# Packed attention with an ELU feed-forward: bit-shifted weights, a refitted planner and split operands

## The chip, the cores and the metric

The kernel runs on one core of a Trainium2 chip. The metric is the device time of one execution in microseconds (us). Before the change three runs took 710.84, 713.93 and 712.98 us; their median is 712.98 us. A smaller time is better.

The core has five engines that run side by side, each through its own instructions in a fixed order: PE (TensorE, the matrix multiplier), DVE (VectorE), ACT (ScalarE), POOL (GpSimd) and SP (SyncE, which here only issues transfers). PEld is PE's loading of the stationary operand.

## The reference

Attention runs twice: 32 packed queries `p` read 576 keys and values, and then the 576 queries `q` read the 32 packed results. A feed-forward with an ELU follows.

```python
# q, k, v: (8, 8, 576, 64) float32; p: (8, 8, 32, 64) float32
def sm_attn(qq, kk, vv):
    s = scale * np.matmul(qq, kk.transpose(0, 1, 3, 2))
    a = np.exp(s - np.max(s, axis=-1, keepdims=True))
    a = a / (np.sum(a, axis=-1, keepdims=True) + 1e-09)
    return np.matmul(a, vv)
p_packed = sm_attn(p, k, v)
out = sm_attn(q, p_packed, p_packed)
x = out.transpose(0, 2, 1, 3).reshape(4608, 512)
h = x @ w_in                                   # w_in: (512, 2048) float64
g = np.where(h > 0.0, h, np.exp(np.minimum(h, 0.0)) - 1.0)
return (g @ w_out).astype(np.float32)          # w_out: (2048, 512) float64
```

The weights arrive as float64, since they are drawn and divided by a float64 root. The chip gets them as pairs of 32-bit words and makes float32 of them itself.

## The kernel before

**Work.** A batch is 576 tokens; there are eight. `w_in` is cut into 16 column blocks of 128 and `w_out` into 16 row blocks, both numbered by `f`. A *step* is one (batch, window, f): the two windows of a batch take 256 and 320 tokens, the 64 odd tokens of an even batch being paired with those of the next batch. A step computes `h` for 128 hidden units (PE), ReLU of -h and exp (ACT), the ELU (DVE), splits the result (ACT cast, DVE subtract), and multiplies it by block `f` of `w_out` (PE, called the *out product* below), accumulating in PSUM.

**h without x.** The packed result `ppT` of a batch is multiplied by `w_in` once (`mstep`, L796), giving `m`; a step then multiplies `m` by the second attention's weights `a` (L1278, L1285, L1048), so `x` is never formed.

**Split operands.** Most products take each float32 operand as a high and a low float32r part and add three products (high x high, high x low, low x high). Where an operand is kept whole, one float32 product is made instead. Before the change this is so for `h` in batches 0 and 1 for `f < 4` (`H_PLAIN = [0, 1]`, L1278, operands `m_hi` and `af`, which lies in the tiles named `k` and `q`) and for the out products of batches 0 and 1 for `f < 4` (`F_PLAIN = 4`, L1395, weights in `w_words`).

**Strassen.** From batch 2's second window to batch 7's first (`strassen_pair`, L1187 and L1048) two steps form a pair, whose out product is a 2x2 block product with seven instead of eight block products. Its sums of weights are made once (`strassen_weights`), stored in `sw_dram` and loaded again for each window. In `S_PLAIN` and `S_PLAINS` stand the pairs of a window that do the plain product with twelve 512-wide matmuls instead of 21 of 256.

**Conversion** (`weights`). Each of the 32 weight blocks (128 x 512 float64) is loaded into one of three `raw` buffers. Before, DVE cuts out the exponent field (`ex`, L312), ACT makes a power of two from it (L319) and a sign from the high word (`sg`, L324), DVE masks the mantissa (`mi`, L327), adds the low word (L333), multiplies power and sign (L340) and multiplies mantissa by that (L350). A `w_out` block is then split (ACT cast, DVE subtract, L363).

**Order.** Every piece of work is an `op` with an urgency, a cost for each engine it may run on, and what it needs. `schedule()` runs through simulated time: whenever an engine is free, the most urgent op that is ready gets it. `GAP` is what is added between two instructions of an engine, `LAG` how much later a result counts as ready. The order so found is written out, engine by engine, and on the chip each engine keeps to it. The first two batches are visited in the order `VISITS` of (batch, window, first f, last f), so that the weight blocks are needed one after another; 64 steps belong to them. `FIRST` orders the first transfers; `T_ATT`, `TM` and the like say how many steps ahead of its use a batch's attention and `mstep` are due; `LOOK` and `LOOK_S` say how many steps the out product stands behind its `h`.

## Time and profile before

| | |
|---|---|
| runs | 710.84, 712.98, 713.93 us; median 712.98 |
| profiled execution, first to last instruction (span) | 710.4 us; its own device time is not given beside it |
| PE busy | 687.2 us, 97% of the span |
| PEld busy | 573.6 us, 81% |
| DVE busy | 587.7 us, 83% |
| ACT busy | 448.1 us, 63% |
| POOL busy | 19.4 us, 3% |
| mean granted PE clock | 0.996 |
| bytes moved | 140.19 MB, 197 GB/s |

Busy time of an engine is time in which at least one of its instructions runs; neighbours overlap by some tens of nanoseconds, so the busy time of a stretch is less than the sum of its instructions. A float32 matmul stands in the trace as two records, a float32r matmul as one. Stages differ much: up to about 31 us the first transfers and the first attention run, up to about 165 us the first two batches with all conversions, then two windows of batch 2 and the Strassen part, and from about 668 us the last window.

### The profile page before, as it was taken

How to read it: one execution, taken by the hardware profiler on the slowest of the kernel's cores; microseconds unless marked ns; L12 is line 12 of the kernel's file. 1: busy time of each engine (PE TensorE's matmuls, PEld its weight loads, DVE VectorE, ACT ScalarE, POOL GpSimd, SP SyncE). 2: the span in 40 equal slices, each digit the busy share in tenths (PEclk: the TensorE clock that was granted, in tenths of full speed). 3: DMA queues.
4: the chain of work that ended last, by engine and by line, in shares of the span. 5: the costliest groups of instructions: out<-in, count | busy, mean ns of one | idle time of the engine just before them, and what ended most of it. 6: DMA issues, size and time to landing. Idle time of an engine off the chain costs nothing.

```text
span 710.4 us, 15186 instructions
## 1 busy us (share of the span) xinstructions
PE 687.2 (97%) x5688; PEld 573.6 (81%) x5688; DVE 587.7 (83%) x1430; ACT 448.1 (63%) x963; POOL 19.4 (3%) x27
## 2 busy tenths in 40 slices
PE   2799999999999999999999999999999999999997
PEld 1444588887777888899889998889888999899986
DVE  6999998888998889776898799866798889977563
ACT  5777788887666666665466555756556655655532
POOL 0000002111021000000000000000000000000000
PEclk9999999999999999999999999999999999999999
DMA  9846555645748845646867897566867887754600
GB/s 354 291 152 216 165 177 117 140 86 124 215 94 208 285 137 179 179 145 195 297 195 260 280 306 230 185 185 203 266 220 243 278 257 226 210 189 138 204 31 30
DMA packets 72553, 140.19 MB, mean 197 GB/s; under 512 B 7200, under 2 KB 16672, under 8 KB 72224
## 3 DMA queue, kind: packets, MB, share of 16 engines
q1 hardware_dynamic: 69456, 133.72, 58.2%
q0 software_dynamic: 3024, 5.51, 5.5%
q8 instruction: 45, 0.74, 0.4%
q14 instruction: 28, 0.23, 0.1%
HBM read 116.92 MB, written 22.28 MB: 196 GB/s over the span
## 4 chain that ended last, share of the span: by engine, by line
PE 93%; DMA 3%; DVE 2%; ACT 1%; issue 0%; SPq 0%; ACTq 0%
PE psum L1187 29%; PE psum L1048 19%; PE psum L1285 8%; PE psum L1409 6%; PE psum L1410 5%; PE psum L1412 5%; PE psum L1007 5%; PE psum L796 4%; PE psum L1395 4%; PE psum L1278 2%; DMA kvq<-in_qT 2%; PE psum L650 2%; PE psum L624 1%; PE psum L695 1%; DMA k<-in_kT 1%; PE psum L554 1%
## 5 line engine op out<-in xcount | busy, mean ns | idle before, releaser
L1187 PE MATMUL psum<-sw,g 128*128 128x256 f32 x816 | 126.0, 282 | 0.0
L1187 PEld LDWEIGHTS psum<-sw,g 128*128 128x128 f32 x816 | 109.9, 188 | 6.5 <-issue 4.7
L1048 PE MATMUL psum<-a_hi,m_hi 128*128 128x320 f32 (+1 forms) x320 | 97.3, 304 | 0.0
L1048 PE MATMUL psum<-a_lo,m_hi 128*128 128x320 f32 (+1 forms) x320 | 95.4, 298 | 0.0
L1048 PE MATMUL psum<-a_hi,m_lo 128*128 128x320 f32 (+1 forms) x320 | 95.3, 298 | 0.0
L1130 DVE TENSOR_TENSOR g<-w,g 128x896 fp32r<-128x896 f32 (+1 forms) x80 | 82.0, 1026 | 13.6 <-ACT g L284 13.1
L284 ACT CAST g<-w 128x896 fp32r<-128x896 f32 (+1 forms) x80 | 71.2, 890 | 23.9 <-DVE w L1121 15.0
L1187 PE MATMUL psum<-wo_a,g 128*128 128x256 f32 (+1 forms) x390 | 72.8, 318 | 0.0
L1121 DVE TENSOR_TENSOR w<-w 128x128 f32<-128x128 f32 (+1 forms) x204 | 68.1, 334 | 5.0
L1060 ACT ACTIVATE e<-psum 128x320 f32<-128x320 f32 x96 | 42.0, 437 | 44.9 <-PE psum L1048 40.1
L1048 PEld LDWEIGHTS psum<-a_hi,m_hi 128*128 128x128 f32 x320 | 60.4, 189 | 11.3 <-ACT e L1063 5.0
L1292 ACT ACTIVATE e<-psum 128x256 f32<-128x256 f32 (+1 forms) x96 | 38.6, 404 | 43.8 <-PE psum L1285 30.2
L1187 PEld LDWEIGHTS psum<-wo_a,g 128*128 128x128 f32 x390 | 58.7, 189 | 8.0 <-issue 2.6
L1048 PEld LDWEIGHTS psum<-a_lo,m_hi 128*128 128x128 f32 x320 | 60.4, 189 | 1.6
L1048 PEld LDWEIGHTS psum<-a_hi,m_lo 128*128 128x128 f32 x320 | 60.4, 189 | 0.0
L1187 PE MATMUL psum<-wo_b,g 128*128 128x256 f32 (+1 forms) x366 | 59.6, 290 | 0.0
L1187 PEld LDWEIGHTS psum<-wo_b,g 128*128 128x128 f32 x366 | 50.9, 188 | 5.3 <-issue 3.1
L1285 PE MATMUL psum<-a_hi,m_hi 128*128 128x256 f32 (+1 forms) x160 | 49.2, 307 | 0.1
L1055 DVE SCALAR_TENSOR_TENSOR w<-e,psum 128x256 f32<-128x256 f32 x96 | 39.6, 413 | 11.5 <-ACT e L1063 11.1
L1063 ACT ACTIVATE e<-e 128x320 f32<-128x320 f32 x96 | 45.3, 472 | 2.5
L1285 PE MATMUL psum<-a_lo,m_hi 128*128 128x256 f32 (+1 forms) x160 | 46.4, 290 | 0.0
L1285 PE MATMUL psum<-a_hi,m_lo 128*128 128x256 f32 (+1 forms) x160 | 46.4, 290 | 0.0
(140 smaller groups left out, 1436.3 us busy)
## 6 DMA issues: line engine op xcount, KB each, us to landing
sw<-sw_dram SPq DMA_DIRECT2D x272, 256.0 KB, 3.6
raw<-in_w_in SPq DMA_DIRECT2D x16, 512.0 KB, 3.9
kvq<-in_v SPq DMA_DIRECT2D x16, 512.0 KB, 5.2
raw<-in_w_out SPq DMA_DIRECT2D x16, 512.0 KB, 3.5
kvq<-in_kT SPq DMA_DIRECT2D x14, 576.0 KB, 5.0
kvq<-in_qT SPq DMA_DIRECT2D x14, 576.0 KB, 5.9
sw_dram<-sw SPq DMA_DIRECT2D x28, 256.0 KB, 4.1
out<-part POOLq DMA_DIRECT2D x21, 256.0 KB, 5.3
```

The costliest lines, as they stand in the source:

```text
L284: (nc.scalar.copy if e == "ACT" else nc.vector.tensor_copy)(out=out, in_=in_)
L1007: nc.tensor.matmul(acc.t, lhsT=gh.t[:, p * P:(p + 1) * P], rhs=wo(f, q), start=f == n == 0, stop=f == NF - 1 and n == 2,)
L1048: nc.tensor.matmul(ps, lhsT=m_b[p].t[:, g, o:o + P], rhs=st.a.t[q][:, g, cols], start=(n == 0), stop=(n == 3 * G - 1),)
L1055: nc.vector.scalar_tensor_tensor(out=out, in0=e_, scalar=-1.0, in1=ps, op0=ALU.add, op1=ALU.max)
L1060: nc.scalar.activation(out=out, in_=ps, func=AF.Relu, scale=-1.0)
L1063: nc.scalar.activation(out=x, in_=x, func=AF.Exp, scale=-1.0)
L1121: nc.vector.tensor_tensor(out=out, in0=x, in1=y, op=o)
L1130: nc.vector.tensor_tensor(out=g_b.all[:, 7 * P:(7 + b1 - b0) * P], in0=blocks(b0, b1), in1=g_b.all[:, :(b1 - b0) * P].bitcast(F32), op=ALU ...
L1187: nc.tensor.matmul(a.t[:, at * H:at * H + rhs.shape[-1]], lhsT=operand(blk, p), rhs=rhs, start=a.first == u and n == k == 0, stop=a.final ...
L1285: nc.tensor.matmul(ps_b.t[:, :n_tok], lhsT=m_b[x].t[:, g, o:o + P], rhs=st.a.t[y][:, g, cols], start=(n == 0), stop=(n == 3 * G - 1),)
L1292: nc.scalar.activation(out=e_b.t[:, :n_tok], in_=ps_b.t[:, :n_tok], func=AF.Relu, scale=-1.0)
L1409: nc.tensor.matmul(a.t, lhsT=g_b.t[0][:, t], rhs=wo(f, 0), start=first, stop=False)
```

## The change

- **Conversion.** A float64's high word, read as float32 and multiplied by 2^-112 on `field`, and the low word scaled on `tail`, are both `scaled` ops that may run on ACT or DVE. `size` shifts the first left by three bits and ors in the second; `signed` ors in the sign bit of the high word and writes the result. Both are DVE instructions on integers. The instructions at L312, L319, L324, L327, L333, L340 and L350 fall away.
- **Split operands.** `F_PLAIN` goes from 4 to 0 and `H_PLAIN` from `[0, 1]` to `[0]`. All out products are split; `h` is whole for batch 0 and `f < 4` alone.
- **Strassen plain pairs.** `S_PLAIN` becomes empty, and `S_PLAINS` lists the windows: there are 13 plain pairs instead of 12 (the new one is pair 4 of batch 6's first window).
- **Planner.** `GAP` and `LAG` are changed; a result needed on the engine that makes it counts as ready when the engine is free. Visits, first transfers and all urgencies get new values. Some bookkeeping of the planner is faster, with no effect on the order.

Counted over the whole program, the matmuls change like this: 36 float32 matmuls of 512 columns (L1395) fall away, and 108 float32r ones of 512 columns come; 8 of 256 and 8 of 320 columns (float32, L1278) fall away, and 24 of 256 and 24 of 320 (float32r) come; 21 of 256 columns become 12 of 512 in the new plain pair. On DVE 160 conversion instructions become 64; 16 steps get a subtraction that they did not have. On ACT 64 conversion instructions stay 64. SP issues 268 loads of `sw` instead of 272.

```diff
-    T_ATT, T_ATT1 = [11.5, 13.5, 14.0, 15.0, 16.0, 16.0], [-12, -11, -11, -10, -10, -9]
-    FIRST = "i0 i1 i2 i3 k v o0 o1 q".split()
-    F_PLAIN, H_PLAIN = 4, [0, 1]
-    S_PLAIN = [0, 7]
+    T_ATT = [9.0, 13.5, 14.0, 15.0, 16.0, 20.0]
+    FIRST = "i0 i1 o0 k i3 v o1 q".split()
+    F_PLAIN = 0
+    H_PLAIN = [0]
+    S_PLAIN = []
...
-    GAP = {"PE": 0.0, "DVE": -0.03, "ACT": 0.02, "DMA": 0.0, "POOL": 0.0, "CTL": 0.0}
-    LAG = {"PE": 0.15, "DVE": 0.1, "ACT": 0.12, "DMA": 2.2, "POOL": 5.0, "CTL": 0.0}
+    GAP = {"PE": 0.0, "DVE": -0.08, "ACT": -0.1, "DMA": 0.0, "POOL": 0.0, "CTL": 0.0}
+    LAG = {"PE": 0.2, "DVE": 0.05, "ACT": 0.05, "DMA": 2.2, "POOL": 5.0, "CTL": 0.0}
...
+                for x, needs in o.next:
+                    x.wait -= 1
+                    if needs:
+                        x.ready = max(x.ready, idle_at[e] if list(x.on) == [e] else o.end)
...
+        def scaled(e, out, in_, by):
+            if e == "ACT":
+                nc.scalar.activation(out=out, in_=in_, func=AF.Copy, scale=by)
+            else:
+                nc.vector.tensor_scalar(out=out, in0=in_, scalar1=by, scalar2=None, op0=ALU.mult)
...
+        def field(e):
+            scaled(e, mi_b.t.bitcast(F32), words()[1].bitcast(F32), 2.0 ** -112)
+        def tail(e):
+            scaled(e, rd_b.t, words()[0], 0.9369 * 2.0 ** -29)
+        def size(e):
             nc.vector.scalar_tensor_tensor(
-                out=mi_b.t.bitcast(F32), in0=words()[0], scalar=2.0 ** -32, in1=mi_b.t,
-                op0=ALU.mult, op1=ALU.add,
+                out=mi_b.t, in0=mi_b.t, scalar=3, in1=rd_b.t,
+                op0=ALU.logical_shift_left, op1=ALU.bitwise_or,
             )
...
             nc.vector.scalar_tensor_tensor(
-                out=out, in0=ms, scalar=2.0 ** -20, in1=pw, op0=ALU.mult, op1=ALU.mult
+                out=out.bitcast(U32), in0=top, scalar=0x80000000, in1=bits,
+                op0=ALU.bitwise_and, op1=ALU.bitwise_or,
             )
...
-        x = op(prio, {"DVE": 0.42}, exponent, [ld], take=[ex_b], use=[raw])
-        s = op(prio, {"ACT": 0.66}, sign, [ld], take=[sg_b], use=[raw])
-        p = op(prio, {"ACT": 0.72}, power, [x], use=[ex_b])
-        m = op(prio, {"DVE": 0.42}, mantissa, [ld], take=[mi_b], use=[raw])
-        w = op(prio, {"DVE": 0.69}, whole, [m], use=[raw, mi_b])
-        g = op(prio, {"DVE": 0.42}, signed, [p, s], use=[ex_b, sg_b])
+        x = op(prio, {"ACT": 0.66, "DVE": 0.42}, field, [ld], take=[mi_b], use=[raw])
+        y = op(prio, {"ACT": 0.66, "DVE": 0.42}, tail, [ld], take=[rd_b], use=[raw])
+        y = op(prio, {"DVE": 0.69}, size, [x, y], use=[mi_b, rd_b])
```

While conversions are left, the planner adds 2 us to the cost of DVE when it chooses between ACT and DVE; all 64 `field` and `tail` instructions stand on ACT.

**Where the order moves, DVE, about 23 to 31 us.** This is batch 0's second softmax, first half: maximum (`mx`), difference, ACT's exp, sum (`sm`), scaling, and the transpose into the tile `k` that the first `h` reads. Before, from the sign product of a conversion on:

```order
L340 TENSOR_TENSOR ex<-ex,sg 128x512
L363 TENSOR_TENSOR wo_a<-w_words,wo_a 128x512
L723 TENSOR_REDUCE sm_374<-tmp 128x18
L523 TENSOR_REDUCE mx<-psum 128x1
L726 TENSOR_SCALAR sm_374<-sm_374 128x18
L729 RECIPROCAL sm_374<-sm_374 128x18
L531 TENSOR_SCALAR nb<-mx 128x1
L523 TENSOR_REDUCE mx<-psum 128x1
L732 TENSOR_TENSOR tmp<-tmp,sm_374 128x576
L531 TENSOR_SCALAR nb<-mx 128x1
L350 SCALAR_TENSOR_TENSOR w_words<-mi,ex 128x512
L745 STREAM_TRANSPOSE k_404<-tmp 128x2x288
```

The same place now:

```order
L340 SCALAR_TENSOR_TENSOR mi<-mi,rd 128x512
L350 SCALAR_TENSOR_TENSOR w_in_sb<-raw,mi 128x4x128
L721 TENSOR_REDUCE sm_310<-tmp 128x18
L724 TENSOR_SCALAR sm_310<-sm_310 128x18
L727 RECIPROCAL sm_310<-sm_310 128x18
L730 TENSOR_TENSOR tmp<-tmp,sm_310 128x576
L743 STREAM_TRANSPOSE k_344<-tmp 128x2x288
L521 TENSOR_REDUCE mx<-psum 128x1
L529 TENSOR_SCALAR nb<-mx 128x1
```

The transpose has moved ahead of batch 1's two maxima, and fewer conversion instructions stand in the softmax.

**PE, about 34 to 42 us**: the end of batch 1's first attention (L650, L676) and the first out products. Before:

```order
L650 MATMUL psum<-kvq,tmp 32x64 x40
L1278 MATMUL psum<-k_404,m_hi 128x256 x2
L676 MATMUL psum<-ident,pp 128x128
L1395 MATMUL psum<-w_words,g 128x512 x2
L1278 MATMUL psum<-k_404,m_hi 128x256 x2
```

Now:

```order
L648 MATMUL psum<-kvq,tmp 32x64 x40
L1282 MATMUL psum<-k_344,m_hi 128x256 x2
L674 MATMUL psum<-ident,pp 128x128
L1282 MATMUL psum<-k_344,m_hi 128x256 x2
L794 MATMUL psum<-w_in_sb,ppT 32x256 x8
L1413 MATMUL psum<-wo_a,g 128x512
L1414 MATMUL psum<-wo_a,g 128x512
```

Step 0's out product (L1395 before, L1413 and the rows behind it now) has moved behind the `h` of step 3 and an `mstep`, and consists of split products.

**ACT, among steps 19 to 22**, where a conversion's instructions are `sg` and `ex` before, `mi` and `rd` now. Before:

```order
L1292 ACTIVATE e<-psum 128x320
L284 CAST wo_b<-mi 128x512
L1298 ACTIVATE e<-e 128x320
L319 ACTIVATE ex<-ex,ebias 128x512
L1292 ACTIVATE e<-psum 128x320
L284 CAST g<-e 128x256
L1298 ACTIVATE e<-e 128x320
L324 ACTIVATE sg<-raw 128x512
```

Now:

```order
L1296 ACTIVATE e<-psum 128x320
L1302 ACTIVATE e<-e 128x320
L322 ACTIVATE mi<-raw 128x512
L301 CAST wo_b<-mi 128x512
L301 CAST g<-e 128x256
L322 ACTIVATE rd<-raw 128x512
L1296 ACTIVATE e<-psum 128x320
L1302 ACTIVATE e<-e 128x320
L322 ACTIVATE mi<-raw 128x512
L322 ACTIVATE rd<-raw 128x512
```

More conversion work stands between the ReLUs of two steps than before: the blocks are converted further ahead of their use.

More of the change, by code (lines that the diff above doesn't have):

```diff
@@ L149, in __init__ @@
             self.ring, self.make, self.n, self.users, self.t = ring, make, n, [], None
+            self.free = False
         def released(self, now):
-            return all(u.end is not None and u.end <= now for u in self.users)
+            self.free = self.free or all(u.end is not None and u.end <= now for u in self.users)
+            return self.free
     class Op:
@@ L172, in schedule @@
     def schedule():
+        for o in ops:
+            o.wait, o.ready, o.next = len(o.deps) + len(o.after), 0.0, []
+        for o in ops:
+            for d in o.deps:
+                d.next.append((o, True))
+            for d in o.after:
+                d.next.append((o, False))
         todo = sorted(ops, key=lambda o: (o.prio, o.n))
         idle_at = {e: 0.0 for e in GAP}
-        now, out, mode = 0.0, [], None
+        now, out, mode, converted = 0.0, [], None, 0
+        conv = set(conv_ops)
         def engine_for(o):
-            if any(d.end is None for d in o.after) or any(
-                d.end is None or d.end > now for d in o.deps
-            ):
+            if o.wait or o.ready > now:
                 return None
@@ L212, in schedule @@
                 todo.remove(o)
+                converted += o in conv
                 break
@@ L378, in weights @@
         last = op(
-            prio, {"DVE": 0.69}, product, [w, g], take=take,
-            use=[mi_b, ex_b] + [b for b in words_b if b not in take],
+            prio, {"DVE": 0.69}, signed, [y], take=take,
+            use=[raw, mi_b] + [b for b in words_b if b not in take],
             after=[w_ready[False, f - 1]] if words_b and f % 2 else [],
@@ L902, in strassen @@
         return S_FIRST <= (b, win) < (B - 1, 1)
+    s_needs = [
+        next((i for i, (b, win, _) in enumerate(order) if strassen(b, win) and u not in plain_in(b, win)), None)
+        for u in range(NF // 2)
+    ]
     def s_need(u):
-        return next((i for i, (b, win, _) in enumerate(order) if strassen(b, win) and u not in plain_in(b, win)), None)
+        return s_needs[u]
     def strassen_weights(u):
```

87 lines of the change are left out of this document (40 added, 47 removed), and 7 rows, old and new, of the table VISITS.

## The prediction

> **What bounds the kernel now.** I read the page's busy times and its chain first, to see which engine sets the end.
>
> ```profile
> span 710.4 us, 15186 instructions
> ...
> PE 687.2 (97%) x5688; PEld 573.6 (81%) x5688; DVE 587.7 (83%) x1430; ACT 448.1 (63%) x963; POOL 19.4 (3%) x27
> ...
> PE 93%; DMA 3%; DVE 2%; ACT 1%; issue 0%; SPq 0%; ACTq 0%
> ```
>
> PE is idle for 710.4 - 687.2 = 23.2 us only, and the chain runs through PE for 93% of the span. So a stage's matmuls, and not DVE's 83%, should set its length. Stretches of time show whether that holds everywhere (columns: stretch and length, then PE, PEld, DVE, ACT busy with their instructions).
>
> ```profile
> 0.00:31.30 31.30, 13.28 (x228) 7.98 (x229) 25.15 (x60) 19.93 (x39) 0.69 (x6) 0.97 0.94 354
> ...
> 34.90:62.45 27.55, 27.27 (x197) 13.21 (x185) 26.13 (x59) 19.16 (x43) 0.00 (x0) 1.00 0.59 192
> 62.45:84.10 21.65, 21.50 (x95) 11.51 (x80) 20.60 (x44) 18.35 (x39) 0.00 (x0) 1.00 0.54 170
> 84.10:124.50 40.40, 40.40 (x249) 32.67 (x248) 36.00 (x89) 33.24 (x81) 3.67 (x4) 1.00 0.53 145
> ...
> 165.00:260.00 95.00, 94.23 (x836) 74.70 (x834) 84.60 (x205) 61.70 (x159) 8.78 (x10) 1.00 0.65 182
> 260.00:660.00 400.00, 399.96 (x3514) 355.68 (x3514) 332.68 (x823) 241.32 (x474) 0.00 (x0) 1.00 0.70 221
> 660.00:710.40 50.40, 46.47 (x289) 41.33 (x287) 26.04 (x69) 19.35 (x48) 0.00 (x0) 0.98 0.23 79
> ```
>
> Of PE's 23.2 idle us, 18.0 lie ahead of 31.3 us and 3.9 in the last stretch. In the 400 us of the Strassen part there is none, so nothing but less PE work shortens that. From 34.9 to 84.1 us (steps 0 to 15) two engines are full together: PE 48.8 and DVE 46.7 of 49.2 us. That is where the change does most, and the question is which of the two sets the pace afterwards.
>
> **PE's work.** Prices come from the chain in order of time (start, length, line, records); a float32 matmul is two records.
>
> ```profile
> 48.78 1.72 PE psum L1395 x4
> 50.50 1.08 PE psum L1278 x4
> ...
> 68.12 0.86 PE psum L1278 x4
> ...
> 302.18 2.79 PE psum L1187 x12
> ...
> 318.28 1.75 PE psum L1048 x12
> ...
> 359.42 1.43 PE psum L1048 x12
> ...
> 405.50 2.47 PE psum L1187 x21
> ```
>
> A 512-wide float32 matmul takes 1.72 / 2 = 0.86 us; a 512-wide float32r one 2.79 / 12 = 0.2325. The 36 of L1395 become 108: 36 x 0.86 = 30.96 against 108 x 0.2325 = 25.1, a saving of 5.9 us. A whole `h` takes 1.08 us (320 columns) or 0.86 (256), a split one 1.75 / 2 = 0.875 or 1.43 / 2 = 0.715; batch 1 has four steps of each, so 4 x (0.205 + 0.145) = 1.4 us go. The new plain pair puts twelve 512-wide in place of twenty-one 256-wide: 2.79 - 2.47 = 0.3 us come. Together PE has 7.0 us less to do, 7.3 of it ahead of step 16, and 687.2 becomes 680.2. If idle time stayed at 23.2 us, the span would be 703.4.
>
> **The start, up to step 0's ELU.** These rows give the first milestones (start, duration, engine, line).
>
> ```profile
> 29.95 0.77 DVE L745 STREAM_TRANSPOSE k<-tmp 128x576 f32<-128x576 f32 x1
> ...
> 31.54 2.58 PE L1278 MATMUL psum<-k,m_hi 128*128 128x256 f32 x8
> ...
> 34.88 0.42 DVE L1301 SCALAR_TENSOR_TENSOR g<-e,psum 128x256 f32<-128x256 f32 x1 [0.25 <-ACT e L1298]
> ...
> 36.78 1.88 PE L1395 MATMUL psum<-w_words,g 128*128 128x512 f32 x4
> ```
>
> The keys' transfer stands behind three weight blocks as before, so PE's first wait stays; I cost the new order of first transfers at nothing, since the first softmax lies between keys and values. Between the first half's transposes and L745 DVE loses ten instructions (five of a conversion, one split, batch 1's two maxima and their two small ones) and gains `size` and `signed`. The group rows price them (busy, mean ns of one).
>
> ```profile
> L333 DVE SCALAR_TENSOR_TENSOR mi<-raw,mi 128x512 f32<-128x512 uint32 x32 | 21.9, 686 | 0.2
> ...
> L327 DVE TENSOR_SCALAR mi<-raw 128x512 uint32<-128x512 uint32 x32 | 13.5, 422 | 0.0
> L312 DVE TENSOR_SCALAR ex<-raw 128x512 uint16<-128x512 uint16 x32 | 13.5, 421 | 3.6 <-DMA raw<-in_w_in 3.6
> L340 DVE TENSOR_TENSOR ex<-ex,sg 128x512 bf16<-128x512 bf16 x32 | 13.4, 418 | 1.9 <-ACT ex L319 1.2 <-ACT sg L324 0.6
> ...
> L523 DVE TENSOR_REDUCE mx<-psum 128x1 f32<-128x576 f32 x6 | 4.5, 751 | 0.9 <-PE psum L513 0.9
> ...
> L350 DVE SCALAR_TENSOR_TENSOR w_in_sb<-mi,ex 128x512 f32<-128x512 f32 x16 | 11.0, 687 | 0.1
> ...
> L319 ACT ACTIVATE ex<-ex,ebias 128x512 bf16<-128x512 uint16 x32 | 22.6, 717 | 2.2 <-DVE ex L312 2.1
> L324 ACT ACTIVATE sg<-raw 128x512 bf16<-128x512 f32 x32 | 21.4, 668 | 7.3 <-DMA raw<-in_w_in 3.9 <-DVE ex L340 1.9 <-DMA raw<-in_w_out 1.5
> ...
> L284 ACT CAST wo_b<-mi 128x512 fp32r<-128x512 f32 x8 | 4.9, 615 | 0.0
> ```
>
> That is 0.42 x 3 + 0.69 x 3 + 0.75 x 2 + 0.25 = 5.1 us out and 1.4 in, some 3 us of DVE time with overlaps taken off; an `mstep` that now stands ahead of the second scores gives 0.5 back, and the first `h` could start about 2.5 us earlier, near 29. It is given back at once: batch 1's maxima now stand behind that transpose, which ends near 30.7 - 2.5 = 28.2, and take 1.8 us; then eleven instructions precede step 0's ELU on DVE (two `size`, two `signed`, a split, two transposes of 0.47, a maximum and a difference of 0.75, two small ones: 6.2 us summed, 5.3 with overlaps). That is 35.3, and 35.6 with the split's wait for ACT, against 34.9. The first out product, which must also await cast and subtraction, comes to about 39 against 36.8. Ends: 33, if the whole 2.5 us are kept, and 37, if the split waits as long as the out product.
>
> **Steps 0 to 15.** Step 16 is the first whose ELU goes to the tile `e` (instances, then shortest, middle and longest in ns, then first and last start).
>
> ```profile
> L1301 DVE SCALAR_TENSOR_TENSOR e<-e,psum x80: 383/415/487, 84.1 to 701.9; 128x256 f32<-128x256 f32 x68, 128x320 f32<-128x320 f32 x12
> ```
>
> The order of DVE, from step 0's ELU up to step 16's (before: 34.9 to 84.1 us), counted by kind and priced with the group rows: before, 102 instructions sum to 54.3 us: 52 for conversions (28.5), 20 for the steps (7.7), 30 for attention and `mstep` (18.1). Now 91 sum to 48.1: 20 for conversions (13.7), 40 for the steps (15.6: twice the instructions, since every step has a subtraction and some a cast on DVE), 31 for the rest (18.8). Before, the 54.3 showed as 46.7 us busy, 0.86 of the sum, so now 41.4. PE needs 48.8 - 7.3 = 41.5 us. Both are full. A stretch with both at 100% would last 41.5 us; with DVE at the 95% that it had before (46.7 / 49.2), 43.6. Between these ends I take 43.6, as the same loop of PE, ACT, DVE, ACT, DVE closes each step. Step 16's ELU then comes at 35.6 + 43.6 = 79.2 instead of 84.1: 4.9 of PE's 7.3 us arrive, 2.4 turn into new idle time of PE.
>
> **ACT, steps 16 to 31** (84.1 to 124.5 us before). Here ACT has 79 instructions that sum to 39.2 us (33.2 busy, 0.85), now 93 that sum to 47.9, or 40.6 busy where PE needs 40.4. The 14 more are 13 conversion instructions and a cast of `m`: blocks taken ahead where ACT had a gap, so I cost them at nothing, with +2.3 us as the other end (40.6 at 95% against 40.4). The new ACT forms are in no row; by rows of the same 512 columns they lie between 0.615 (L284) and 0.717 us (L319), and I take 0.668 (L324), which also reads every second word. `size` and `signed` lie between 0.42 (L327) and 0.69 (L350); I take 0.69.
>
> A rule speaks against this. The Trainium skill ("ScalarE: Activation LUTs", Rules for kernel authors) says that a multiplication by a constant belongs on VectorE rather than on ScalarE. The trace agrees on the price, 422 ns (L327) against 668 (L324). By the rule the 20 scalings that ACT makes up to step 16 would add 20 x 0.42 x 0.86 = 7 us to a DVE that is full there, and the 4.9 would be gone; between steps 16 and 31 it would instead relieve ACT. The sum above goes by the program as it is.
>
> From step 16 on PE stays the bound; the Strassen part changes by the 0.3 us of the plain pair. Its weight sums, its loads (issued earlier, four fewer) and the last window (3.9 us idle) I leave at nothing: DVE is at 83% there and the transfers at 70%.
>
> **Sum**: -4.9 + 0.3 = -4.6 us. The span becomes 705.8. The page gives the profiled execution no time beside its span; the median lies 2.6 us above that span. I put the sum against the median: 712.98 - 4.6 = 708.4.
>
> **Rivals.** (a) *PE's saving comes through whole*, and the early transpose brings a little: step 0 at 33 to 34.9 and 41.5 us for the steps put step 16 at 74.5 to 76.4 instead of 84.1, which is -7.4 to -9.3 with the plain pair, so 703.7 to 705.6, a little less if later waits shrink too. For it: DVE loses 15 us of conversions here and may convert later. Against it: two full engines in a closed loop. (b) *The pace stays with DVE and ACT*, so the change does not do what less PE work should: step 0 at 37 and 44 to 45 us for the steps (ACT also takes over casts) put step 16 at 81 to 82, -3.1 to -2.1; with 0.3 for the plain pair and up to 2.3 for ACT that is -2.8 to +0.5, so 710.2 to 713.5, and more if one late block joins in. For it: 95% on DVE, 40.6 of 40.4 on ACT. (c) *Slower*: ACT becomes the bound through its new forms. All 64 lie ahead of step 48. If ACT has no slack there, each 0.13 us above 0.668 adds 64 x 0.13 = 8.3 us, which makes 716.7. So it decides from 0.80 us on, above every 512-column row of ACT; a long wait for a late weight block would look the same. The rows speak against it.
>
> **Numbers.** A measurement of this kernel tells about 0.5% from no change, 3.6 us: faster is below 709.4, slower above 716.5. The forecast (706 to 710.5) gets 0.47, of which 0.38 lie below 709.4; (a) 0.18; (b) 0.27; (c) 0.08. Faster 0.38 + 0.18 = 0.56, same 0.09 + 0.27 = 0.36, slower 0.08. A range of 703 to 713 leaves out (c), the part of (b) above 713 (0.07) and of (a) below 703 (0.04).
>
> **What would show it.** Right: PE busy near 680; step 0's ELU near 35.6 and step 16's near 79; idle time of PE between 31 and 80 us of 2 to 3 us where before there was 0.5; the Strassen part as full as before; DVE busy some 30 us less. Wrong: PE waiting for ACT between 80 and 125 us, `mi` and `rd` rows above 0.72 us, PE waits in the Strassen part (new loads or sums late), or a step 0 several us off 35.6, which shifts all that follows.

## The result and the profile after

The changed kernel takes 733.87 us (median of four runs, 731.98 to 734.51) where the kernel before, on the same chip, takes 713.45 us: a ratio of 1.029, 95% interval 1.026 to 1.032. The forecast was 708.4. The profiled execution took 731.98 us, 2.1 us more than its span.

The page of the changed kernel: span, busy times, and the chain that ended last.

```profile
span 729.9 us, 15216 instructions
...
PE 690.2 (95%) x5731; PEld 580.2 (79%) x5731; DVE 578.8 (79%) x1349; ACT 457.6 (63%) x983; POOL 19.3 (3%) x27
...
PE 49%; DVE 31%; ACT 11%; issue 4%; DMA 4%; SPq 0%; DVEq 0%; ACTq 0%
```

No engine's share stands out more than before, DVE's has even fallen from 83% to 79%. But the chain ran through PE for 93% of the span and now does so for 49%; 31% of it are DVE. DVE is not the busiest engine; it is the late one.

The place shows when the kernel is cut into four stages, at the starts of three ELU rows in DVE's timeline (step 0, step 16, and step 79, the last one ahead of the Strassen part; these are L1301 before and L1305 after). Lengths in us:

| | to step 0's ELU | steps 0 to 15 | steps 16 to 79 | Strassen part and last window |
|---|---|---|---|---|
| before | 34.9 | 49.2 | 167.8 | 458.5 |
| after | 36.0 | 47.1 | 169.9 | 476.9 |

Up to step 79 the two kernels differ by about 1 us; the loss of 18.4 us lies behind it, where the prediction had put 0.3. The stretches of the Strassen part and of the last window, of the kernel before:

```profile
251.93:666.47 414.54, 414.50 (x3606) 368.92 (x3605) 344.36 (x856) 249.68 (x494) 0.00 (x0) 1.00 0.69 217
666.47:710.40 43.93, 40.00 (x241) 35.13 (x240) 21.37 (x53) 15.65 (x38) 0.00 (x0) 0.98 0.19 67
```

And of the kernel after, with the stretch of steps 0 to 15 ahead of them:

```profile
36.02:83.10 47.08, 43.95 (x322) 32.30 (x315) 43.61 (x93) 38.97 (x92) 0.00 (x0) 0.97 0.52 172
252.96:686.94 433.98, 423.14 (x3609) 370.14 (x3608) 349.19 (x835) 257.80 (x509) 0.00 (x0) 1.00 0.63 205
686.94:729.90 42.96, 38.84 (x228) 33.71 (x226) 21.10 (x56) 14.50 (x37) 0.00 (x0) 0.98 0.17 58
```

PE has nearly the same matmul records there (3847 before, 3837 after, the two rows added), the granted clock is the same in both, and the transfers' share fell. Yet PE is idle for 10.8 us inside the Strassen part (before: 0.04), and it is "busy" for 7.5 us more over the two rows. The second number is waiting too: a matmul's record is longer than the distance to the next (0.31 us for a 320-column one at a distance of 0.15), so a wait of a tenth of a microsecond disappears in the record before it. From the start of a group of three matmuls on `sw` (L1187, now L1191) to the start of the row behind it in PE's timeline there are now 0.43 us in the mean, before 0.37, though the records are as long as before (0.28 us). The corrected kernel below has the same matmuls as this one and is busy for 455.1 us over the two rows, not 462.0. The Trainium skill says this of the view ("Perfetto Trace Analysis", Identifying the Most-Contended Engine: the matmul busy share is not a good measure of how near the engine is to its limit); the two rows agree.

Whom PE waits for in that stretch (waiting line, releaser, us in total, times, longest); before, the same view has no row at all:

```profile
PE psum L1050 <- DVE half_sb L1057: 2.5, 7, 0.7
PE psum L552 <- DVE m_lo L807: 1.8, 2, 1.3
PE psum L1050 <- DVE part L1215: 1.5, 1, 1.5
PE psum L1050 <- DVE w L1057: 1.4, 2, 1.1
```

In the first and the last row, 3.9 us together, PE stands in front of `h` (L1050) because the PSUM bank that it wants is still held by an ELU (L1057) that DVE has not reached; the other two wait for other late results of DVE. No load of `sw` is among these rows.

### The profile page after: what moved, and what is told of

The parts are those of the page before. It is cut to its first block, busy times and chain, and to the rows that moved or that the text cites. A ratio compares the mean times of both kernels' runs of the same rounds, so it can differ in the third digit from the quotient of the medians.

```text
span 729.9 us, 15216 instructions
## 1 busy us (share of the span) xinstructions
PE 690.2 (95%) x5731; PEld 580.2 (79%) x5731; DVE 578.8 (79%) x1349; ACT 457.6 (63%) x983; POOL 19.3 (3%) x27
## 4 chain that ended last, share of the span: by engine, by line
PE 49%; DVE 31%; ACT 11%; issue 4%; DMA 4%; SPq 0%; DVEq 0%; ACTq 0%
PE psum L1191 14%; PE psum L1050 9%; PE psum L1289 6%; DVE w L1123 5%; DVE g L1132 4%; PE psum L1413 4%; PE psum L1414 4%; PE psum L1416 4%; DVE w L1057 3%; PE psum L794 3%; DVE part L1215 2%; ACT g L301 2%; PE psum L1009 2%; DVE m_lo L807 2%; PE psum L648 1%
## 5 line engine op out<-in xcount | busy, mean ns | idle before, releaser
L1191 PE MATMUL psum<-sw,g 128*128 128x256 f32 x804 | 124.2, 283 | 0.7 <-issue 0.4
L1191 PEld LDWEIGHTS psum<-sw,g 128*128 128x128 f32 x804 | 108.1, 188 | 8.0 <-issue 5.2
L1050 PE MATMUL psum<-a_hi,m_hi 128*128 128x320 f32 (+1 forms) x320 | 98.9, 309 | 7.1 <-DVE half_sb L1057 2.5
L1050 PE MATMUL psum<-a_hi,m_lo 128*128 128x320 f32 (+1 forms) x320 | 95.4, 298 | 0.0
L1050 PE MATMUL psum<-a_lo,m_hi 128*128 128x320 f32 (+1 forms) x320 | 95.4, 298 | 0.0
L1050 PEld LDWEIGHTS psum<-a_hi,m_hi 128*128 128x128 f32 x320 | 60.4, 189 | 23.7 <-issue 7.8
L1191 PE MATMUL psum<-wo_a,g 128*128 128x256 f32 (+1 forms) x390 | 73.2, 320 | 0.6 <-DVE gh L301 0.3
L1123 DVE TENSOR_TENSOR w<-w 128x128 f32<-128x128 f32 (+1 forms) x201 | 67.6, 336 | 6.7
L1057 DVE SCALAR_TENSOR_TENSOR w<-e,psum 128x256 f32<-128x256 f32 x96 | 39.9, 417 | 37.8 <-ACT e L1065 37.3
L1191 PEld LDWEIGHTS psum<-wo_a,g 128*128 128x128 f32 x390 | 58.5, 188 | 11.6 <-issue 3.0
L1296 ACT ACTIVATE e<-psum 128x256 f32<-128x256 f32 (+1 forms) x96 | 38.4, 400 | 41.6 <-PE psum L1289 33.7
L1050 PEld LDWEIGHTS psum<-a_lo,m_hi 128*128 128x128 f32 x320 | 60.4, 189 | 0.8
L1305 DVE SCALAR_TENSOR_TENSOR e<-e,psum 128x256 f32<-128x256 f32 (+1 forms) x96 | 41.0, 428 | 25.2 <-ACT e L1302 24.7
L1191 PE MATMUL psum<-wo_b,g 128*128 128x256 f32 (+1 forms) x369 | 60.8, 294 | 0.0
L1050 PEld LDWEIGHTS psum<-a_hi,m_lo 128*128 128x128 f32 x320 | 60.4, 189 | 0.0
L1191 PEld LDWEIGHTS psum<-wo_b,g 128*128 128x128 f32 x369 | 52.2, 188 | 4.5 <-issue 2.1
L1289 PE MATMUL psum<-a_hi,m_hi 128*128 128x256 f32 (+1 forms) x176 | 53.1, 302 | 2.4 <-DVE half_sb L1305 1.1
L1289 PE MATMUL psum<-a_lo,m_hi 128*128 128x256 f32 (+1 forms) x176 | 51.1, 291 | 0.0
L1289 PE MATMUL psum<-a_hi,m_lo 128*128 128x256 f32 (+1 forms) x176 | 51.1, 291 | 0.0
```

Of the source, the lines that this page charges most:

```text
L1050: nc.tensor.matmul(ps, lhsT=m_b[p].t[:, g, o:o + P], rhs=st.a.t[q][:, g, cols], start=(n == 0), stop=(n == 3 * G - 1),)
L1057: nc.vector.scalar_tensor_tensor(out=out, in0=e_, scalar=-1.0, in1=ps, op0=ALU.add, op1=ALU.max)
L1123: nc.vector.tensor_tensor(out=out, in0=x, in1=y, op=o)
L1191: nc.tensor.matmul(a.t[:, at * H:at * H + rhs.shape[-1]], lhsT=operand(blk, p), rhs=rhs, start=a.first == u and n == k == 0, stop=a.final ...
L1289: nc.tensor.matmul(ps_b.t[:, :n_tok], lhsT=m_b[x].t[:, g, o:o + P], rhs=st.a.t[y][:, g, cols], start=(n == 0), stop=(n == 3 * G - 1),)
L1296: nc.scalar.activation(out=e_b.t[:, :n_tok], in_=ps_b.t[:, :n_tok], func=AF.Relu, scale=-1.0)
```

## What DVE does there

The instructions are nearly those of before; their neighbours are not. DVE's timeline (start, duration) of the changed kernel, in a pair of the Strassen part that shares DVE with a softmax:

```profile
411.27 0.68 DVE L1057 SCALAR_TENSOR_TENSOR w<-w,psum 128x512 f32<-128x512 f32 x1
411.98 1.08 DVE L1123 TENSOR_TENSOR w<-w 128x128 f32<-128x128 f32 x3
412.98 0.75 DVE L721 TENSOR_REDUCE sm<-tmp 128x18 f32<-128x576 f32 x1
413.75 0.18 DVE L724 TENSOR_SCALAR sm<-sm 128x18 f32<-128x18 f32 x1
413.97 0.27 DVE L727 RECIPROCAL sm<-sm 128x18 f32<-128x18 f32 x1
414.27 0.76 DVE L730 TENSOR_TENSOR tmp<-tmp,sm 128x576 f32<-128x576 f32 x1
```

The kernel before, around its softmax sum at the same time:

```profile
416.54 0.74 DVE L723 TENSOR_REDUCE sm<-tmp 128x18 f32<-128x576 f32 x1
417.20 0.21 DVE L1055 SCALAR_TENSOR_TENSOR half_sb<-e,psum 128x64 f32<-128x64 f32 x1
417.33 0.17 DVE L726 TENSOR_SCALAR sm<-sm 128x18 f32<-128x18 f32 x1
417.53 0.27 DVE L729 RECIPROCAL sm<-sm 128x18 f32<-128x18 f32 x1
```

Before, an ELU of another step stands between the softmax sum and the instruction that reads it. It starts 0.66 us behind the sum, 0.08 ahead of that one's end: neighbours that don't depend on each other overlap by that much. After, L724 stands directly behind L721, which it reads, and starts 0.77 us behind it, 0.02 after the end. The sums L1123 read the ELU ahead of them and start 0.03 after its end. So a dependent neighbour costs about 0.1 us more than an independent one. In the changed kernel the ELU and the sums of a pair, and the four small steps of a softmax, stand back to back.

That is what the new planner asks for. It sets `GAP` of DVE to -0.08, which is right for independent neighbours, and its readiness line lets a result be used on the same engine as soon as the engine is free: 0.08 us *before* the producing instruction ends. The ELU of 0.69 us is planned with its sums 0.61 us behind it; the chip does it in 0.71. The kernel before counted a result as ready 0.1 us *after* the end, and so mostly found something else to do first. My theory (theory 1 below) became: **the planner now believes that dependent neighbours on DVE cost nothing extra, writes them back to back, DVE falls behind the plan, and PE pays for it.**

The sum over all of DVE's groups (count times mean, kept apart by shape) shows the same: 667.5 us of durations were 587.7 us busy before, a ratio of 0.880; now 634.8 are 578.8, a ratio of 0.912. DVE lost 32.7 us of instructions, but only 8.9 us of busy time, where the prediction had looked for some 30. A count of neighbours shows it too: 449 times (before 243) an instruction on DVE starts 0 to 0.06 us behind the end of the one ahead of it, and 680 times (before 969) it starts ahead of that end, by 0.08 us in the mean.

## Experiments

Rival theories were: the new urgencies of the Strassen part are bad (2), or the new conversion and the split operands are (3). In what follows *constants* means `GAP`, `LAG` and the readiness line; *tables* means visits, transfers' order, urgencies and the two small numbers `STAY` and `SWITCH`; *work* means conversion and split operands. The table at the end has all stages.

**Old constants in the changed kernel.** Tables and work stay new.

```diff
-    GAP = {"PE": 0.0, "DVE": -0.08, "ACT": -0.1, ...}
-    LAG = {"PE": 0.2, "DVE": 0.05, "ACT": 0.05, ...}
+    GAP = {"PE": 0.0, "DVE": -0.03, "ACT": 0.02, ...}
+    LAG = {"PE": 0.15, "DVE": 0.1, "ACT": 0.12, ...}
-                        x.ready = max(x.ready, idle_at[e] if list(x.on) == [e] else o.end)
+                        x.ready = max(x.ready, o.end)
```

> The changed kernel, its planner taken back to the old GAP, LAG and readiness (a result counts as ready after LAG on its own engine too); work, tables and urgencies stay new. Theory 1 (the new intervals are too short, above all for a chain of DVE instructions that need one another, so the order leaves PE waiting in the Strassen part): 706 to 716 us, PE idle in the Strassen part under 3 us. Theory 2 (the new tables put the work in bad places): 727 to 736 us, PE idle in the Strassen part near 11 us as in the changed kernel. Theory 3 (the new conversion or the split operands cost it): 727 to 736 us.

727.09 us, ratio 1.021 (1.016 to 1.026). The stages from the Strassen part on come back by 12.9 us (476.9 to 464.0), but step 79 is 7.9 us later, perhaps because the visits and urgencies of the first two batches don't fit these constants. Theory 1 had expected 706 to 716 us; the whole came out where theories 2 and 3 had put it, and only PE's idle time in the Strassen part (3.5 us) is near what theory 1 had said. The constants carry 12.9 of the 18.4 us behind step 79, not all of them.

**New constants in the kernel before.** The same lines the other way; work and tables stay old.

> The kernel before, with only the planner's new GAP, LAG and readiness; conversion, operands, tables and urgencies stay old. Theory 1: 722 to 735 us, with PE waiting for DVE in the Strassen part. Theory 2: 709 to 717 us, the Strassen part as full as before. Theory 3: 709 to 717 us.

751.16 us, ratio 1.053 (1.051 to 1.055). The constants alone cost more than the whole change, and more than the 722 to 735 us that theory 1 had expected: 17.3 us up to step 79 and 19.8 behind it. The longest waits of PE in its Strassen part are for DVE again:

```profile
PE psum L1054 <- DVE half_sb L1061: 4.8, 7, 1.6
PE psum L1054 <- DVE gh L992: 2.4, 1, 2.4
PE psum L556 <- DVE m_lo L811: 1.5, 2, 0.8
```

Since nothing else of the change is in this kernel, the late DVE does not come from the conversion, the splits or the tables.

**New work in the kernel before**, with old constants and tables.

```diff
-    F_PLAIN, H_PLAIN = 4, [0, 1]
+    F_PLAIN = 0
+    H_PLAIN = [0]
...
+        x = op(prio, {"ACT": 0.66, "DVE": 0.42}, field, [ld], take=[mi_b], use=[raw])
+        y = op(prio, {"ACT": 0.66, "DVE": 0.42}, tail, [ld], take=[rd_b], use=[raw])
+        y = op(prio, {"DVE": 0.69}, size, [x, y], use=[mi_b, rd_b])
```

> The kernel before, with only the new conversion and the new operand splits; planner constants, tables and urgencies stay old. Theories 1 and 2: 704 to 712 us, since 7 us of matmuls are gone and the Strassen part stays full. Theory 3: 725 us or more.

717.82 us, ratio 1.006 (1.003 to 1.009), all of it ahead of step 79; the rest lasts 458.3 us as before. So theory 3 explains nothing of the Strassen part. But theories 1 and 2 had expected 704 to 712 us: PE's smaller work by itself, under old tables, is no gain.

**Old tables in the changed kernel**, with new constants and work.

```diff
-    T_ATT = [9.0, 13.5, 14.0, 15.0, 16.0, 20.0]
-    FIRST = "i0 i1 o0 k i3 v o1 q".split()
-    T_SW = 15
+    T_ATT, T_ATT1 = [11.5, 13.5, 14.0, 15.0, 16.0, 16.0], [-12, -11, -11, -10, -10, -9]
+    FIRST = "i0 i1 i2 i3 k v o0 o1 q".split()
+    S_FIRST, T_SW, T_SL, T_SE, LOOK_S = (2, 1), 17, 10, 5, 6.0
...
```

> The changed kernel with all tables and urgencies of the kernel before (visits, first transfers, attention, Strassen); work and planner constants stay new. Theory 1: 722 to 735 us, PE waiting in the Strassen part. Theory 2: 704 to 714 us. Theory 3: 725 us or more.

744.05 us, ratio 1.043 (1.041 to 1.045): step 79 comes 12.1 us later than with the new tables, and the rest takes the same 476.9. Theory 2 by itself falls: under the new constants the new tables are the better ones up to step 79 and no worse behind it. The time is above theory 1's band here too (722 to 735).

**Which of the constants?** Three kernels with a single run each, all made from the kernel before. The readiness line alone:

```diff
-                        x.ready = max(x.ready, o.end)
+                        x.ready = max(x.ready, idle_at[e] if list(x.on) == [e] else o.end)
```

> The kernel before with one line of the planner new: an op that needs a result made on its own engine may follow as soon as that engine is free by the plan. GAP, LAG, tables and work are old. The measure is the Strassen part, from the last ELU of batch 2's first window to the first of the last window: 414.5 us before, 433 with all new constants. Theory A (a DVE instruction that needs the one before it really starts some 0.1 us later than planned, and the plan no longer puts other work between): 420 to 430 us. Theory B (only GAP and LAG matter): 414 to 417. Theory C (the urgencies fit one plan only, and any other plan costs): 420 to 430 here and also in the run with slack added.

730.78 us, the Strassen part 422.9; behind step 79 it is 8.3 us longer than before. `GAP` and `LAG` alone:

> The kernel before with the new GAP and LAG alone; readiness, tables and work are old. Strassen part by theory A: 416 to 424 us (LAG of DVE 0.05 where the trace shows 0.1, but the chain of DVE instructions still gets it). Theory B: 428 to 435. Theory C: 420 to 430.

728.43 us, the Strassen part 421.6; 7.0 us longer there. And a control that moves them the other way, so that the planner believes in more time than the chip takes:

```diff
-    GAP = {"PE": 0.0, "DVE": -0.03, "ACT": 0.02, ...}
-    LAG = {"PE": 0.15, "DVE": 0.1, "ACT": 0.12, ...}
+    GAP = {"PE": 0.0, "DVE": 0.0, "ACT": 0.04, ...}
+    LAG = {"PE": 0.15, "DVE": 0.15, "ACT": 0.15, ...}
```

> The kernel before with a planner that errs the other way: GAP of DVE 0 and of ACT 0.04, LAG 0.15 for both; readiness, tables and work are old. Strassen part by theories A and B: 414 to 418 us, since a plan with too long intervals leaves the chip nothing to wait for. Theory C: 420 to 430, as with any other constants.

723.45 us, the Strassen part 417.9; 3.3 us longer behind step 79, 7.4 ahead of it. So other constants cost something here even where they are cautious, perhaps since the old tables were chosen with the old ones, and some 3 us of each of the two runs above may be that. The halves add up to 15.3 us and together make 19.8: both wrong at once is worse than their sum.

DVE's neighbours tell the two halves apart. The readiness line alone makes 474 of the late starts counted above (0 to 0.06 us behind the end; 243 before) and a ratio of busy time to sum of 0.905. `GAP` and `LAG` alone make 273 and 0.881, and the slack 235 and 0.882, hardly other than before. So the chains on DVE come from the readiness line; what `GAP` and `LAG` cost by themselves has another cause, which no run here shows.

**The theory's own repair.** In the changed kernel two numbers are corrected: a result used on its own engine is ready 0.03 us after the end, and one of DVE's used elsewhere 0.1 us after (ACT starts 0.11 after the end of an L1123 that it waits for). `GAP` stays at -0.08. The timeline contradicts the first number plainly, the second only at times: over the 113 times that ACT sat idle for a result of DVE in the changed kernel it starts 0.03 us after that result's end in the median, and 0.09 us or more after it in the slowest tenth. No run corrects one of the two alone.

```diff
-    LAG = {"PE": 0.2, "DVE": 0.05, "ACT": 0.05, ...}
+    LAG = {"PE": 0.2, "DVE": 0.1, "ACT": 0.05, ...}
-                        x.ready = max(x.ready, idle_at[e] if list(x.on) == [e] else o.end)
+                        x.ready = max(x.ready, now + cost + 0.03 if list(x.on) == [e] else o.end)
```

> The changed kernel with its new GAP, but a result on the same engine counts as ready 0.03 us after its full cost, and LAG of DVE is 0.1, as the trace shows both. Tables and work are new. Strassen part by theory A: 416 to 424 us and the whole 712 to 722; theories B and C: 428 to 436 and 727 or more.

711.68 us in a single run. The same program, timed:

> The changed kernel with only the planner's readiness and DVE's LAG set to what the trace shows (0.03 us after the full cost on the same engine, 0.1 across engines), now timed against the kernel before. If theory A is the cause, 709 to 715 us, a ratio of 0.995 to 1.002, 20 us under the changed kernel; if the one look was luck, 716 or more.

712.38 us, ratio to the kernel before 0.999 (0.997 to 1.001). Two numbers of the planner take back 21.5 us of the changed kernel's time (733.87 to 712.38), as theory A had expected. Its page, its stretches from step 79 on, and PE's waits in its Strassen part:

```profile
PE 681.4 (96%) x5731; PEld 579.1 (82%) x5731; DVE 565.5 (80%) x1353; ACT 447.6 (63%) x979; POOL 19.3 (3%) x27
```

```profile
249.06:669.62 420.56, 418.56 (x3624) 371.60 (x3623) 340.26 (x832) 255.21 (x515) 0.00 (x0) 1.00 0.67 213
669.62:710.20 40.58, 36.51 (x214) 31.84 (x212) 20.38 (x54) 14.36 (x37) 0.00 (x0) 0.98 0.12 41
```

```profile
PE psum L794 <- DVE part L1215: 1.1, 1, 1.1
PE psum L622 <- ACT tmp L579: 0.5, 1, 0.5
PE psum L1191 <- DVE e L1057: 0.2, 1, 0.2
```

Of the 3.9 us of waits for L1057 0.2 are left. DVE has 1353 instructions instead of 1349, which sum to 637.7 us instead of 634.8, and is busy for 565.5 instead of 578.8: the ratio is 0.887, and the late starts are 262 instead of 449. Its timeline shows why (L711 reads L708's result, L1123 that of L1057, L724 that of L721):

```profile
409.77 0.75 DVE L708 TENSOR_REDUCE mx<-tmp 128x18 f32<-128x576 f32 x1
410.44 0.68 DVE L1057 SCALAR_TENSOR_TENSOR w<-w,psum 128x512 f32<-128x512 f32 x1
411.04 0.75 DVE L711 TENSOR_TENSOR tmp<-tmp,mx 128x576 f32<-128x576 f32 x1
411.70 1.07 DVE L1123 TENSOR_TENSOR w<-w 128x128 f32<-128x128 f32 x3
...
413.70 0.75 DVE L721 TENSOR_REDUCE sm<-tmp 128x18 f32<-128x576 f32 x1
414.36 0.41 DVE L1057 SCALAR_TENSOR_TENSOR w<-e,psum 128x256 f32<-128x256 f32 x1
414.69 0.17 DVE L724 TENSOR_SCALAR sm<-sm 128x18 f32<-128x18 f32 x1
```

Softmax and feed-forward alternate, and the same 0.68 us ELU that held its successor for 0.71 us in the changed kernel lets it start after 0.60.

**The parts of the work.** The conversion alone, in the kernel before:

> The kernel before with the new conversion alone: DVE has 40 us less to do, PE the same matmuls; planner, tables and operands are old. Theory P (PE bounds, DVE's relief is worth nothing and a changed plan costs a few us): 713 to 719. Theory Q (DVE and ACT pace the first 84 us, so relief shows): step 16's ELU 3 us or more earlier than 84.1 and 707 to 711.

716.48 us, ratio 1.004 (1.003 to 1.006), as theory P had it. The split operands alone:

> The kernel before with the new operand splits alone: PE has 7 us less, DVE and ACT have 16 subtractions and casts more among steps 0 to 15, where DVE was busy for 95%; planner, tables and conversion are old. Theory P: step 16's ELU 5 us or more earlier than 84.1, 705 to 709 us. Theory Q: it comes at 84 or later and PE idles there for 4 us or more, 713 to 722.

713.30 us, ratio 1.001 (0.999 to 1.002), near theory Q: PE is busy for 682.2 us instead of 687.2, and the saving comes to nothing. PE idles for 3.7 us in steps 0 to 15 (before: 0.4), where DVE stands at 98%, and for 3.4 in steps 16 to 63 (0.8). Its longest waits there are for an ELU and, in front of the out product, for a copy on ACT and a subtraction on DVE:

```profile
PE psum L1293 <- DVE e L1309: 1.5, 1, 1.5
PE psum L1417 <- ACT part L286: 1.0, 1, 1.0
PE psum L1417 <- DVE m_lo L811: 0.9, 1, 0.9
```

Conversely the conversion frees DVE (82% in steps 0 to 15) where PE has as much to do as ever; those steps even take 52.7 us instead of 49.2. Either half removes time from one of two engines that are full together. Under the old tables both halves together are no better (the kernel with new work, PE idle for 8.2 us in steps 0 to 63); under new tables with corrected constants (the kernel above) step 79 comes 2.9 us earlier than before.

**What was still open: the last microseconds.** The corrected kernel's stages from step 79 on last 461.1 us, 2.7 more than before. (Its Strassen part alone is 6.0 us longer and its last window 3.3 shorter, but 27 matmul records that stood in the last window now stand ahead of it; the two are better compared together.) Old Strassen tables under corrected constants:

```diff
-    T_SW = 15
-    T_SL = 16
+    S_FIRST, T_SW, T_SL, T_SE, LOOK_S = (2, 1), 17, 10, 5, 6.0
...
```

> The changed kernel with the measured readiness and LAG, and with the old tables for the Strassen part (attention and m of batches 3 to 7, plain pairs, loads). If the new Strassen tables are what keeps its Strassen part at 420.4 us, that part takes 414 to 417 and the whole 704 to 709; if the old tables fit only the old constants, 420 to 428 and 711 to 720.

715.67 us, ratio 1.003 (1.001 to 1.005), the Strassen part 422.4; 466.3 us from step 79 on, so the old tables are the worse ones here. The corrected constants in the kernel before, with its tables and work:

> The kernel before with its own conversion, splits and tables; the planner's constants are the new ones with the two corrections of the run before (a dependent instruction on the same engine ready 0.03 us behind the end, DVE's lag 0.1). With all new constants this kernel took 751.2 us and 433.1 us in the Strassen part, with its own constants 713 and 414.5. Theory 1 (the uncorrected dependence is the cause, whatever the tables): Strassen part 414.5 to 419, whole 713 to 722. Theory 2 (tables fit one set of constants, and any other set costs): Strassen part 420 to 424 as in the control with slack (417.9) or worse, whole 722 to 735.

722.69 us, ratio 1.012 (1.009 to 1.015): 28.5 of the 37.7 us that the uncorrected constants cost this kernel come back; 4.7 us stay behind step 79 and 6.5 ahead of it, like the control's 3.3 and 7.4. The Strassen part itself takes 418.1 us, within what theory 1 had expected of it, though the whole is 0.7 us beyond its band. What is left is of the size that the control's constants cost under the same tables.

Two attempts at a kernel that beats both change the constants at 235 us of the planner's time, from corrected to old. With old Strassen tables behind that point:

```diff
+                gap, lag = (GAP, LAG) if now < 235 else (GAP_2, LAG_2)
+                        x.ready = max(x.ready, now + cost + 0.03 if list(x.on) == [e] and now < 235 else o.end)
```

> New conversion, splits and first-two-batch tables with the corrected constants up to 235 us of the planner's time; from there the Strassen tables and the constants of the kernel before. Theory 1+2 (each part wants constants and tables that fit each other): step 79 near 249 as in the corrected kernel, Strassen part 414.5 to 416 as in every kernel with old constants and old Strassen tables, tail 41 to 44: 706 to 710 us, faster than both. Rival (the Strassen part ends late because its first steps start from another state of engines and buffers): Strassen part 419 to 423, whole 711 to 716.

711.76 us, ratio 0.998 (0.996 to 1.000): step 79 is 2.4 us earlier than before, and the rest lasts 459.9, 1.4 longer. The Strassen part of 416.0 us is as I had expected it, but the whole is above the 706 to 710; the gain is too small to be told from none. With new Strassen tables:

> As the switched kernel, but with the new Strassen tables under the old constants. If the tables fit only the constants they were chosen with, the Strassen part takes about 424 us as in the kernel with new tables and old constants throughout (424.5), whole 715 to 718; if that run's loss came from its late first batches, 415 to 418, whole 706 to 711.

714.06 us in a single run, 463.8 from step 79 on, as in the changed kernel with old constants throughout (464.0): by this run it was not the late start that cost 5.5 us there but new tables under old constants.

One profiled execution of each kernel, in us; a second one of the corrected kernel (711.68 us) has stages within 0.4 us of the first. The stages are cut as in the first table; PE's idle time is that of the stretch from step 79's ELU to the last window's first. A time with no interval is a single run.

| kernel | time | ratio to before | step 0 | 0 to 15 | 16 to 79 | from 79 on | PE idle |
|---|---|---|---|---|---|---|---|
| before | 713.45 | | 34.9 | 49.2 | 167.8 | 458.5 | 0.0 |
| after | 733.87 | 1.026 to 1.032 | 36.0 | 47.1 | 169.9 | 476.9 | 10.8 |
| after, old constants | 727.09 | 1.016 to 1.026 | 37.6 | 51.6 | 171.7 | 464.0 | 3.5 |
| after, old tables | 744.05 | 1.041 to 1.045 | 42.8 | 47.4 | 174.8 | 476.9 | 11.3 |
| before, new constants | 751.16 | 1.051 to 1.055 | 44.0 | 50.3 | 174.9 | 478.3 | 11.8 |
| before, readiness line | 730.78 | | 42.7 | 47.1 | 171.0 | 466.8 | 5.1 |
| before, GAP and LAG | 728.43 | | 37.1 | 50.2 | 173.5 | 465.5 | 5.5 |
| before, more slack | 723.45 | | 36.2 | 51.8 | 171.3 | 461.8 | 5.3 |
| before, new work | 717.82 | 1.003 to 1.009 | 37.2 | 49.3 | 171.2 | 458.3 | 0.1 |
| before, conversion | 716.48 | 1.003 to 1.006 | 36.6 | 52.7 | 165.4 | 459.5 | 0.3 |
| before, splits | 713.30 | 0.999 to 1.002 | 35.8 | 49.7 | 167.3 | 458.4 | 0.1 |
| before, corrected | 722.69 | 1.009 to 1.015 | 38.4 | 51.9 | 168.2 | 463.2 | 1.9 |
| after, corrected | 712.38 | 0.997 to 1.001 | 36.3 | 47.9 | 164.9 | 461.1 | 2.0 |
| same, old Strassen tables | 715.67 | 1.001 to 1.005 | 36.5 | 47.9 | 164.8 | 466.3 | 5.1 |
| switched, old Strassen tables | 711.76 | 0.996 to 1.000 | 36.3 | 48.2 | 165.0 | 459.9 | 1.2 |
| switched, new Strassen tables | 714.06 | | 35.0 | 47.7 | 165.5 | 463.8 | 3.5 |

## The prediction, step by step

**PE's work: right in size.** The corrected kernel has all the new matmuls and is 681.4 us busy (forecast 680.2). That the changed kernel, with the same matmuls, shows 690.2 is waiting inside records, as read above.

**The start: right.** Step 0's ELU came at 36.0 us (forecast 35.6, ends 33 to 37), and on the path that the forecast took: the transpose into `k` ends at 28.0 (forecast 28.2), and the first out product starts at 40.2 (about 39).

**The price of the new instructions: right,** and with it the mechanism of rival (c) excluded. The groups of the changed kernel (busy, mean ns, idle ahead):

```profile
L322 ACT ACTIVATE mi<-raw 128x512 f32<-128x512 f32 x32 | 21.5, 671 | 3.4 <-DMA raw<-in_w_in 3.0
L322 ACT ACTIVATE rd<-raw 128x512 uint32<-128x512 uint32 x32 | 21.2, 661 | 0.1
L340 DVE SCALAR_TENSOR_TENSOR mi<-mi,rd 128x512 uint32<-128x512 uint32 x32 | 22.1, 691 | 12.1 <-ACT rd L322 11.2
L350 DVE SCALAR_TENSOR_TENSOR mi<-raw,mi 128x512 uint32<-128x512 uint32 x16 | 11.0, 689 | 0.3
```

671 and 661 ns stand against the 668 taken, 691 and 689 against 690. No run put these scalings on DVE, so what that would have cost stays open. The time fell on the side of (c) for a reason that (c) did not hold.

**Steps 0 to 15: mis-sized.** Forecast 43.6 us, measured 47.1, so step 16's ELU came at 83.1 instead of 79.2. PE was busy for 43.95 us of it, not 41.5, and idle for 3.1, not 2.1 (43.6 - 41.5). On DVE the forecast counted right and overlapped wrong: 91 instructions sum to 48.1 us as forecast, but are busy for 43.6 and not 41.4, 0.91 of the sum and not the 0.86 taken over from before. That is the back-to-back order again. Two stretches hold most of the loss (the number behind POOL's is the granted clock):

```profile
36.00:42.00 6.00, 6.00 (x61) 4.22 (x54) 5.66 (x14) 4.80 (x14) 0.00 (x0) 0.80 0.64 209
...
48.00:54.00 6.00, 4.06 (x17) 2.59 (x16) 5.83 (x15) 3.06 (x7) 0.00 (x0) 1.00 0.45 173
```

In the first the clock was granted at 0.80, worth some 1.2 us (an estimate, a fifth of 6 us). In the second PE does 4.1 us of work while DVE is full with a softmax whose steps stand back to back: there DVE set the pace at 97%. The corrected kernel has full clock there and still takes 47.9, with PE busy for 45.0 and DVE for 43.4, so the term would have been too small with a good plan too. How much of PE's 45.0 us is waiting inside records was not settled.

**Steps 16 to 79 at nothing, +2.3 as the other end:** measured +2.1, with PE idle for 2.2 us instead of 0.8. Corrected, the stage is 2.9 us *shorter* than before, so this was the plan and not ACT's fuller load.

**"From step 16 on PE stays the bound; the Strassen part changes by the 0.3 us of the plain pair": the step that failed.** It became 18.4 us longer. I left it at nothing because DVE stood at 83% there and the transfers at 70%. The order that keeps DVE ahead of PE was itself an output of the lines that I had read as a change of numbers, and I counted instructions there without asking what each *place* in the order assumes about its neighbour. What was needed stood there: the diff puts a reader 0.08 us ahead of the end of what it reads, and in the trace of before the reader of a direct predecessor's result (L729 behind L726: 417.53 against 417.33 + 0.17) starts after the end. The list of what would prove it wrong did name PE's waits in the Strassen part, but with the loads or the weight sums as the cause; it was DVE's results, ELUs above all.

**The expected gain of 4.6 us.** Corrected, PE is busy for 6.3 us less up to step 79 (226.4 against 232.7), 3.5 of them come back as idle time, and step 79 is 2.9 us earlier. From there on 2.7 us are lost again. 0.3 of these are the plain pair; the rest was not settled beyond this: it depends on which tables meet which constants (459.9 to 466.3 us over the combinations run), and PE's own work is the same. Shares of single constants can't be told better than to the 3 us that the control shows.

## What to carry to other kernels

Where a planner writes the order, its model of time is part of the kernel: check each of its numbers against two kinds of neighbours in the trace, those that depend on each other and those that don't, since one number for both moves the wrong instructions together. A planner that counts a dependent result as ready a little late keeps independent work between the two, while one that counts it early writes chains that the engine then waits on. More slack in all the numbers is no free safety: here, under tables chosen for other numbers, it cost 10 us (723.45 against 713.16 us, single runs). When two engines are full together, time taken from one of them may only become its idle time, as it did here; and new constants want new tables, so vary them apart before judging either.

## What the runs showed of the hardware

On DVE a neighbour that does not wait for the instruction ahead starts 0.07 to 0.09 us before that one's end (L721 to L1057 in the corrected kernel: 0.66 us at a duration of 0.75), one that reads its result 0.02 to 0.04 us after it (L721 to L724 in the changed one: 0.77). The Trainium skill has the first half ("Perfetto Trace Analysis", Optimizing Scalar/DVE Operations: the write acknowledgement of an instruction overlaps with the next one), and the trace agrees for independent neighbours. For dependent ones it does not. "VectorE: DVE Perf Modes" (The DRAIN you can't avoid) states that a semaphore after each instruction cost nothing extra in its measurement. In these rows an instruction that must wait for its direct predecessor's result starts about 0.1 us later than one that need not; a semaphore between independent neighbours was not tried here. Between the changed and the corrected kernel, whose DVE instructions are almost the same, 190 more starts ahead of the neighbour's end (870 instead of 680) at 0.08 us each make some 16 us; DVE is busy for 13.3 us less although its instructions sum to 2.9 us more.
